# Attention and two feed-forward layers in one kernel: the written-out order of all instructions is replaced by another, and the planner's prices with it

## The chip, the core and the metric

One core of a Trainium2 chip runs one program. The metric is the device time of one execution in microseconds (us). Three executions of the kernel before took 1180.26, 1184.04 and 1186.45 us; the median, 1184.04, is the time before.

## What is computed

Attention over 4 batches of 12 heads, 448 positions, head size 64, with q and k normalised; its output, as 1792 rows of 768, goes through one feed-forward layer (768 to 2048 to 768) and a gated one (768 to 1536 to 768). All inputs and the output are float32.

```python
q_n, k_n = rmsnorm(q, g_q), rmsnorm(k, g_k)
attn = softmax(scale * q_n @ k_n.T)
x = (attn @ v).transpose(0, 2, 1, 3).reshape(B * S, H * D)
h = x @ w_in                       # 1792x768 @ 768x2048
x = (h * sigmoid(h)) @ w_out       # 2048x768
g = x @ w_gate                     # 768x1536
return (g * sigmoid(g) * (x @ w_val)) @ w_out2
```

## The kernel before, in words

Nearly every float32 operand is split into two float16 halves, a high part and a remainder, and a product is three float16 matmuls. Five engines share the work: PE multiplies; ACT, DVE and POOL take exponentials, maxima, splits and scalings; SP issues nearly all DMAs. Weights are loaded, scaled to a power of two and split (`bring`, `split`, `convert`) while attention runs. Attention of the four batches overlaps with the first feed-forward layer of the batch before it (`softmax_pair`, `pv_pair`, `ffn1_h`, `ffn1_o`). The second layer goes over four blocks of rows, of 512, 512, 384 and 384. The first block uses plain products (`ffn2_gv`); the others use a scheme with seven products for eight (`ffn2_seven`), for which sums of weights are made on the chip: `weight_sums` loads pieces of the gate and value weights again from `y2d` (L1281), combines them on DVE (L1288 to L1291), splits them (L967, L979) and stores them to `s2d` (L1293), from which `ffn2_seven` loads them (L1515). `make_parts` does the like for the last weights: loads from `w2d` (L1480), DVE (L1482 to L1489), ACT (L1486, L1491), stores to `t2d` (L1494). Its ACT results go into one buffer, `th`, so that ACT's next L1486 waits until the three stores before it have landed. `ffn2_seven` takes its products from the accumulators with ACT (L1549) and DVE (L1546), applies the gate (L1562 to L1587) and writes halves (L1586, L1589). `ffn2_out` multiplies (L1643), scales and adds (L1652 to L1656) and stores rows (L1668).

Each step is handed to a planner, `Plan.add`, with the engines that may do it, a price in ns on each, what it reads and writes, and a due time. `Plan.emit` then plays the program through at build time: at each moment the engine that is free first takes, of what is ready, the step that is due first, and its instructions are written out in that order. So the order on every engine, and where there is a choice the engine too, is fixed by prices and due times. The chip runs each engine's list in that order and waits on semaphores; it doesn't reorder. A DMA is a `move(hold, service, lead, ...)`: SP is held for `hold`, and the transfer lands after the transfers ahead of it and its own `lead` and `service`. Where the plan leaves PE idle for more than `GAP` ns, it fills the gap with matmuls whose result nobody reads (L1811).

Due times come from formulas plus offsets of a search that was run beforehand and left in `TUNE`: `OFF` by kind of step, `FINE` by one step, `NUDGE` by number of the step. Letters in `TUNE` (`A`, `D`, `P` for ACT, DVE, POOL) say which engines may do a step; where there are several, `emit` picks.

The planner before also knows that PE's instruction stream is fetched in pieces: with `FETCH = (128, 73, 1500.0)` it counts the matmuls that it writes out and, at the 73rd and every 128 after that, makes whatever transfer comes next land 1500 ns later:

```python
if fetches and t0 >= fetches[0]:
    fetches.pop(0)
    served += bump
```

Of the kernel before, what the change touches and what calls it, by code (L numbers as in the profile page):

```python
# [26 lines left out]
    WIY=('DP', 'D', 'AP', 'AP', 'DP', 'ADP', 'AD', 'AP'),  # L27
    WOY=('AD', 'A', 'AD', 'ADP', 'AD', 'D', 'ADP', 'AP'),
# [27 lines left out]
    TK='AD',
    NB=('ADP', 'AD', 'ADP'),
    WIH=('AP', 'A', 'AD', 'DP', 'A', 'AD', 'ADP', 'AP'),
    WIL=('D', 'P', 'E', 'D', 'DP', 'D', 'DP', 'DP'),
    WOH=('D', 'ADP', 'A', 'AP', 'AP', 'ADP', 'ADP', 'AD'),  # L60
    WOL=('E', 'E', 'E', 'E', 'E', 'E', 'E', 'E'),
    WIS=('P', 'P', 'AP', 'P', 'D', 'P', 'A', 'AP'),
    WOS=('D', 'D', 'D', 'D', 'D', 'D', 'D', 'D'),
# [320 lines left out]
def t_ptt(n):  # L384
    return 2.1 * n + 50
# [1461 lines left out]
```

## Time and profile before

| | |
|---|---|
| median of three executions | 1184.04 us (1180.26 to 1186.45) |
| the profiled execution | 1184.59 us, of which the span from first to last instruction 1182.8 |
| busy in the span | PE 1140.7, DVE 917.6, ACT 749.7, POOL 260.6 us |
| mean granted TensorE clock | 0.996 of full speed |
| PE time in matmuls that only fill gaps (L1811) | 24.7 us, 86 of them |
| DMA | 222.59 MB, mean 188 GB/s |

Times are in us from the first instruction unless ns is said. An engine's idle time matters only where it reaches PE, which is busy for 96% of the span; a row's last part in brackets is the idle time of the engine just before it and what ended that.

### The profile page before, as it was taken

The numbers are of one execution on the slowest core, as the hardware profiler recorded it, in microseconds if no ns is written. First come the engines' busy times: TensorE is split into PE (matmuls) and PEld (weight loads), VectorE is DVE, ScalarE is ACT, GpSimd is POOL, SyncE is SP. The second block draws the span as 40 slices with busy tenths as digits, with TensorE's granted clock in tenths as the row PEclk, the third lists the DMA queues.
The fourth block names the chain that finished last, engine by engine and source line by source line (L and its number), as shares of the span: only waits on it lengthen the run. The fifth ranks groups of instructions, "written<-read, shape, count | busy, mean of one in ns | idle before, by whom it ended". The sixth has DMA issues, their size and how long they took to land.

```text
span 1182.8 us, 20080 instructions
## 1 busy us (share of the span) xinstructions
PE 1140.7 (96%) x7400; PEld 675.8 (57%) x7400; DVE 917.6 (78%) x1762; ACT 749.7 (63%) x1288; POOL 260.6 (22%) x231
## 2 busy tenths in 40 slices
PE   8999998999999999999999999999999899999998
PEld 4444544454444445454555554445688668987995
DVE  5989988988588876885379978877999866774773
ACT  4888978887599856995468667574356531441440
POOL 4585222245344524531031021000000000000000
PEclk9999999999999999999999999999999899999999
DMA  9555755689979997776756878646787675463432
GB/s 212 160 132 146 242 202 154 111 193 189 201 158 180 184 203 163 149 139 136 260 176 200 295 250 298 217 157 199 237 255 249 231 247 168 161 190 117 168 130 67
DMA packets 271315, 222.59 MB, mean 188 GB/s; under 512 B 187120, under 2 KB 246000, under 8 KB 271216
## 3 DMA queue, kind: packets, MB, share of 16 engines
q1 hardware_dynamic: 271056, 221.10, 68.0%
q8 instruction: 58, 0.95, 0.3%
q14 instruction: 41, 0.34, 0.1%
q10 hardware_dynamic: 160, 0.20, 0.0%
HBM read 140.44 MB, written 38.14 MB: 151 GB/s over the span
## 4 chain that ended last, share of the span: by engine, by line
PE 34%; DMA 9%; DVE 7%; ACT 5%; issue 2%; SPq 1%; POOL 1%; ACTq 0%; DVEq 0%; POOLq 0%
PE ps L1529 12%; PE ps L1643 9%; PE ps L1155 5%; PE ps L1195 4%; DMA ATT<-y2d 3%; PE ps L1407 2%; DMA ATT<-in_moe_w_out_dram 2%; DMA t2d<-ATT 1%; DMA ATT<-s2d 1%; DMA ATT<-in_moe_w_val_dram 1%; DVE ATT L979 1%; PE ps L951 1%; ACT ATT L1034 1%; DMA ATT<-x2d 1%; PE ps L841 1%
## 5 line engine op out<-in xcount | busy, mean ns | idle before, releaser
L1155 PE MATMUL ps<-XT,W 128*128 128x448 f16 x1152 | 232.5, 352 | 2.5 <-ACT FD L1161 2.3
L1195 PE MATMUL ps<-G,W 128*128 128x448 f16 x1152 | 233.4, 352 | 1.5 <-ACT FD L1199 1.1
L1155 PEld LDWEIGHTS <-W 128*128 128x128 f16 x1152 | 112.0, 98 | 108.1 <-issue 7.9
L1195 PEld LDWEIGHTS <-W 128*128 128x128 f16 x1152 | 111.9, 98 | 108.1 <-issue 6.0
L1529 PEld LDWEIGHTS <-ATT 128*128 128x128 f16 x1458 | 130.8, 99 | 16.4 <-issue 6.5
L1529 PE MATMUL ps<-XT,ATT 128*128 128x192 f16 (+1 forms) x972 | 122.0, 257 | 6.8 <-ACT G L1549 5.7
L860 ACT ACTIVATE ER<-ps,ST 128x448 f32<-128x448 f32 x144 | 102.0, 712 | 12.2 <-DVE ATT L884 5.0
L1643 PEld LDWEIGHTS <-G 128*128 128x128 f16 x720 | 70.3, 98 | 46.9 <-issue 0.3
L1643 PE MATMUL ps<-W,G 128*128 128x384 f16 x528 | 95.8, 326 | 0.1
L851 DVE TENSOR_REDUCE ST<-ps 128x2 f32<-128x896 f32 (+1 forms) x96 | 91.7, 965 | 5.3 <-PE ps L820 2.5
L884 DVE SCALAR_TENSOR_TENSOR ATT<-ER,ST,ATT 128x448 f16<-128x448 f32 x114 | 81.1, 729 | 3.5 <-ACT ATT L876 2.8
L1407 PE MATMUL ps<-XT,W 128*128 128x512 f16 x360 | 81.6, 379 | 1.3 <-ACT FD L1199 0.6
L1529 PEld LDWEIGHTS <-W 128*128 128x128 f16 x810 | 73.0, 98 | 8.3 <-issue 3.1
L1529 PE MATMUL ps<-XT,W 128*128 128x192 f16 (+1 forms) x540 | 73.2, 256 | 2.7 <-DVE ATT L1656 1.8
L1529 PE MATMUL ps<-ER,ATT 128*128 128x192 f16 (+1 forms) x486 | 66.5, 257 | 0.0
L1407 PEld LDWEIGHTS <-W 128*128 128x128 f16 x360 | 35.2, 98 | 43.1 <-issue 3.0
L841 PE MATMUL ps<-ATT 128*128 128x448 f16 x216 | 55.3, 353 | 3.7 <-ACT ER L860 2.9
L694 POOL TENSOR_TENSOR ST<-ST 128x14 f32<-128x14 f32 x20 | 55.9, 2797 | 1.4
L1174 DVE SCALAR_TENSOR_TENSOR G<-FD,ST,G 128x448 f16<-128x448 f32 x64 | 46.7, 743 | 7.0 <-POOL G L1168 4.6
L1546 DVE TENSOR_TENSOR FD<-ps,FD 128x192 f32<-128x192 f32 (+3 forms) x90 | 41.3, 464 | 11.2 <-PE ps L1529 9.2
L1656 DVE SCALAR_TENSOR_TENSOR ATT<-ps,ST,ATT 128x384 f32<-128x384 f32 x46 | 27.6, 614 | 23.9 <-ACT ATT L1652 23.3
L951 PE MATMUL ps<-ATT 128*64 128x448 f16 x396 | 42.2, 355 | 4.0 <-DMA ATT<-ATT 4.0
(283 smaller groups left out, 2123.8 us busy)
## 6 DMA issues: line engine op xcount, KB each, us to landing
ATT<-s2d SPq DMA_DIRECT2D x36, 768.0 KB, 4.3
ATT<-in_moe_w_out_dram SPq DMA_DIRECT2D x24, 768.0 KB, 6.6
ATT<-t2d SPq DMA_DIRECT2D x36, 384.0 KB, 3.6
W<-in_moe_w_in_dram SPq DMA_DIRECT2D x16, 768.0 KB, 6.5
ATT<-in_moe_w_gate_dram SPq DMA_DIRECT2D x12, 768.0 KB, 5.7
ATT<-in_moe_w_val_dram SPq DMA_DIRECT2D x12, 768.0 KB, 5.5
y2d<-ATT SPq DMA_DIRECT2D x24, 384.0 KB, 2.9
ATT<-y2d SPq DMA_DIRECT2D x12, 768.0 KB, 5.8
```

What stands on the lines that cost most here:

```text
L694: op(POOL, 2600, lambda: nc.gpsimd.tensor_tensor(st["r"], st["r"], half, ALU.pow), shared=False, r=["half"], w=[("r", i)], due=due)
L841: nc.tensor.matmul(out=sp[:, u, 0:S], lhsT=T[:, 0, t, :], rhs=T[:, a, :, 64 * h:64 * h + 64], start=(a == 1), stop=(a == 2))
L851: op(DVE, 1.04 * S * nt + 65, lambda sp=sp, top=top, nt=nt: nc.vector.tensor_reduce(top, sp[:, 0:nt, 0:S], AX.X, ALU.max, negate=True), r= ...
L860: op(ACT, 705, lambda e=e, u=u, t=t, sp=sp, own=own: nc.scalar.activation(e, sp[:, u, 0:S], AF.Exp, bias=st["nb"][:, t:t + 1], scale=1.0 i ...
L884: DVE: (t_stt(S), lambda e=e, hi=hi, lo=lo, r1=r1: nc.vector.scalar_tensor_tensor(lo, e, r1, hi, ALU.mult, ALU.subtract), True),
L951: nc.tensor.matmul(out=PS_X[64 * h:64 * h + 64, 0:S], lhsT=vv[:, h, b, :], rhs=PT[:, b].rearrange("p t c -> p (t c)")[:, S * h:S * h + S], ...
L1155: nc.tensor.matmul(out=ps[:, 0:S], lhsT=w[:, a, kk], rhs=xt1((b * HP + kk) % NX, x), start=(kk == 0 and s == 0), stop=(kk == KD - 1 and s ...
L1174: DVE: (t_stt(S), lambda gt=gt, hi=hi, lo=lo, s1=s1: nc.vector.scalar_tensor_tensor(lo, gt, s1, hi, ALU.mult, ALU.subtract), True),
L1195: nc.tensor.matmul(out=ps[:, 0:S], lhsT=w[:, a, P * m:P * m + P], rhs=GV1[:, f, x], start=(f == 0 and s == 0), stop=(f == NF1 - 1 and s == 2))
L1407: nc.tensor.matmul(out=ps[:, 0:n], lhsT=w[:, aa, kk], rhs=xt2(kk, x)[:, 0:n], start=(kk == 0 and s == 0), stop=(kk == KD - 1 and s == 2))
L1529: nc.tensor.matmul(out=ps[:, h * o:h * o + h], lhsT=w[:, aa, kk], rhs=XW[kk][:, c:c + h], start=(kk == 0 and s == 0), stop=(kk == KH - 1 a ...
L1643: nc.tensor.matmul(out=ps[:, bank, 0:384], lhsT=lh[a], rhs=rh[b], start=(x == 0 and (bank, a, b) != (1, 1, 0)), stop=(x == m - 1 and (bank ...
```

## The change

The order is another one. `FINE` and `NUDGE` hold other numbers throughout (the same steps, other due times), and many letters differ. The fetch model is taken out: `FETCH`, the counting of matmuls and the bump are gone, so that the build no longer knows when a fetch comes. The search that found the new numbers was run beforehand, with each candidate judged by ten plays in each of which a tenth of the transfers land late, every transfer in exactly one; none of that search is in the kernel. Nine prices differ. No step of the computation is added or removed, and no wait is added by hand.

```diff
-    FETCH = (128, 73, 1500.0)
...
-                if fetches and t0 >= fetches[0]:
-                    fetches.pop(0)
-                    served += bump
...
-            if e == PE:
-                streamed += self.products[i]
-                while streamed >= fetch:
-                    fetches.append(t0)
-                    fetch += step
...
-        op(POOL, 295, lambda: nc.gpsimd.tensor_scalar(st["r"], ...      # L693, L753
+        op(POOL, 190, lambda: nc.gpsimd.tensor_scalar(st["r"], ...
-            POOL: (t_ptt(448) + 250, ... raw[:, 1], rk3 ...              # L700
+            POOL: (t_ptt(448) - 75, ...
-        op(PE, 440, mm, r=["psz", "id"] + ek, ...                        # L904
+        op(PE, 475, mm, ...
-                op(PE, *((835, scores_0) if n < N0 ...                   # L820
+                op(PE, *((925, scores_0) if n < N0 ...
-            POOL: (t_pts(n) + t_ptt(n) + 96, lo_pool)}), ...             # L974 and L975, in split
+            POOL: (t_pts(n) + t_ptt(n) + 440, lo_pool)}), ...
-        move(420, 2900, 1700, ... in_=y2d ...                            # L1281
+        move(420, 2600, 2650, ...
-        move(490, 1800, 1500, ... out=s2d ...                            # L1293
+        move(490, 1900, 2180, ...
-            move(370, 2300, 2050, ... in_=s2d ...                        # L1515
+            move(370, 2150, 2150, ...
-                move(400, 1300, 1500, ... out=rows, in_=src ...          # L1668
+                move(400, 800, 1540, ...
```

Of the letters, those that the text below speaks of (the others are changed in the same manner):

```diff
-    WOY=('AD', 'A', 'AD', 'ADP', 'AD', 'D', 'ADP', 'AP'),
+    WOY=('AD', 'A', 'A', 'DP', 'ADP', 'ADP', 'D', 'P'),
-    WOH=('D', 'ADP', 'A', 'AP', 'AP', 'ADP', 'ADP', 'AD'),
+    WOH=('AP', 'A', 'A', 'DP', 'ADP', 'A', 'AD', 'AP'),
-    SU='DP',
+    SU='D',
-    TSH='ADP',
-    TSL='A',
-    XU='D',
+    TSH='A',
+    TSL='AP',
+    XU='DP',
```

`TSH` is L1486, `TSL` is L1491, `XU` the additions of L1445, `SU` the remainder of the weight sums (L979 in that place), `WOY` and `WOH` steps of the first output weights.

## Rows read from the trace of the kernel before

**Rows 1.** Busy time by engine in five stretches; then clock, DMA share, GB/s.

```profile
0.00:210.00 210.00, 194.57 (x1005) 95.00 (x1006) 177.27 (x273) 167.31 (x294) 92.80 (x74) 1.00 0.61 176
210.00:500.00 290.00, 280.58 (x1614) 139.63 (x1613) 233.48 (x474) 226.94 (x430) 124.05 (x117) 1.00 0.87 175
500.00:850.00 350.00, 346.90 (x1865) 177.61 (x1864) 266.90 (x495) 227.26 (x335) 43.78 (x40) 1.00 0.70 213
850.00:935.00 85.00, 77.06 (x661) 65.64 (x660) 79.23 (x167) 47.11 (x75) 0.00 (x0) 0.96 0.77 241
935.00:1179.00 244.00, 241.61 (x2263) 197.93 (x2261) 160.45 (x357) 81.09 (x157) 0.00 (x0) 1.00 0.49 162
```

**Rows 2.** PE by line and form: the matmuls that fill gaps.

```profile
L1811 PE MATMUL ps<-NI 128*128 128x512 f16 x86 | 24.7, 412 | 5.1 <-POOL NI L572 5.1
```

**Rows 3.** Timeline of ACT and PE around 920: start, duration, engine, instruction.

```profile
919.79 0.78 ACT L1486 ACTIVATE ATT<-W,ST 128x576 f16<-128x576 f32 x1 [1.43 <-DMA t2d<-ATT]
...
925.10 0.38 ACT L1549 ACTIVATE G<-ps 128x256 f32<-128x256 f32 x1 [0.47 <-DVE W L1580]
...
925.53 0.80 PE L1529 MATMUL ps<-XT,ATT 128*128 128x256 f16 x3 [4.86 <-ACT G L1549]
```

**Rows 4.** DMA view of 914 to 920: queue, and issues with us to landing.

```profile
q8 instruction: 1, 0.02, 1.4%
...
t2d<-ATT SPq DMA_DIRECT2D x3, 96.0 KB, 4.2
```

**Rows 5.** DMA issues of the whole span: count, KB, median us to landing.

```profile
ATT<-y2d SPq DMA_DIRECT2D x12, 768.0 KB, 5.8
s2d<-ATT SPq DMA_DIRECT2D x12, 768.0 KB, 6.7
...
t2d<-ATT SPq DMA_DIRECT2D x36, 96.0 KB, 3.0
...
out_dram<-ATT SPq DMA_DIRECT2D x9, 384.0 KB, 2.8
```

**Rows 6.** DMA queues, whole span: packets, MB, share of 16 engines' span.

```profile
q8 instruction: 58, 0.95, 0.3%
```

**Rows 7.** DMA view of 1080 to 1086: GB/s in 40 slices, queue, issue.

```profile
GB/s 0 0 0 0 0 0 0 0 0 335 348 430 369 369 348 348 21 0 0 0 0 0 20 0 20 0 20 41 20 20 20 0 0 0 0 0 0 0 0 0
...
q8 instruction: 1, 0.02, 1.9%
...
out_dram<-ATT SPq DMA_DIRECT2D x1, 384.0 KB, 4.6
```

**Rows 8.** Timeline of PE, an early and a late stall.

```profile
297.33 0.95 PE L951 MATMUL ps<-ATT 128*64 128x448 f16 x8 [1.22 <-DMA ATT<-ATT]
...
1086.59 0.41 PE L1529 MATMUL ps<-XT,W 128*128 128x192 f16 x3 [1.21 <-DVE ATT L1656]
```

**Rows 9.** DMA view of 293 to 298, its queue row.

```profile
q8 instruction: 1, 0.02, 1.1%
```

**Rows 10.** Busy times and clock of two stretches after that stall.

```profile
925.00:930.00 5.00, 4.46 (x22) 3.08 (x22) 5.00 (x11) 3.15 (x5) 0.00 (x0) 0.50 0.44 160
930.00:935.00 5.00, 5.00 (x41) 4.18 (x40) 3.71 (x8) 1.40 (x2) 0.00 (x0) 0.86 0.48 170
```

**Rows 11.** POOL by line and form: count, busy us, mean ns, idle before.

```profile
L974 POOL TENSOR_SCALAR ATT<-ATT,ST 128x768 f32<-128x768 f32 x6 | 7.6, 1261 | 64.8 <-DVE ATT L968 31.0 <-ACT W L967 12.2 <-DVE W L968 8.1
L975 POOL TENSOR_TENSOR W<-ATT,W 128x768 f16<-128x768 f32 x4 | 7.9, 1986 | 0.3
```

**Rows 12.** POOL's L693 and L700 alone: duration ns min/median/max.

```profile
L693 POOL TENSOR_SCALAR ST<-ST x20: 208/209/1649, 57.7 to 489.5; 128x14 f32<-128x14 f32 x20
...
L700 POOL TENSOR_TENSOR ATT<-ATT,ST x12: 936/1000/1907, 273.3 to 494.1; 128x448 f32<-128x448 f32 x12
```

**Rows 13.** Waits by engine: us in total, times, longest.

```profile
PE ps L795 <- ACT W L798: 4.1, 9, 1.1
PE ps L951 <- DMA ATT<-ATT: 4.0, 4, 1.3
...
ACT ATT L1486 <- DMA t2d<-ATT: 8.7, 4, 6.1
```

More of the change, by code (lines that the diff above doesn't have):

```diff
@@ L145, in __init__ @@
         self.filler = None
-        self.products = {}
     def bank(self, key, ap):
@@ L158, in short, with add @@
         self.drains[j] = i
-    def add(self, alts, r=(), w=(), due=0.0, late=0.0, table=None, cont=False, count=3):
+    def add(self, alts, r=(), w=(), due=0.0, late=0.0, table=None, cont=False):
         i = len(self.ops)
-        self.products[i] = count
         for key in set(r) | set(w):
@@ L241, in emit @@
         served = 0.0
-        step, fetch, bump = self.FETCH
-        streamed, fetches = 0, []
         opened = {}
@@ L332, in emit @@
                     self.fill[i] = 213.0 * times
-                    streamed += times
             if i in self.taken:
@@ L843, in scores @@
                                 rhs=T[:, a, :, 64 * h:64 * h + 64], start=(a == 1), stop=(a == 2))
[L844 to L845 removed]
+                op(PE, *((925, scores_0) if n < N0 else (600, scores_1) if n < HP else (600, scores) if t == J // 2 else (380, scores)),
+                   r=tk, w=[sk[u]], due=due - 1000)
             t0 = tiles[0]
@@ L919, in row_scales @@
         ps, pk = psf()
-        op(PE, 800, lambda: nc.tensor.matmul(out=ps[:, 0:S], lhsT=BO, rhs=DR_0, start=True, stop=True), r=["vl", "vh"], w=[pk], due=due - 500, count=2)
+        op(PE, 800, lambda: nc.tensor.matmul(out=ps[:, 0:S], lhsT=BO, rhs=DR_0, start=True, stop=True), r=["vl", "vh"], w=[pk], due=due - 500)
         rt, rtk = ft()
@@ L936, in pv @@
                             start=(b == 0), stop=(b == 3))
-            op(PE, 3300, pv, r=[(V_0K[n > 0], u) for u in range(3)] + [("pt0", n % 2, t) for t in range(J)], w=["psx"], due=due - 1000, count=16)
+            op(PE, 3300, pv, r=[(V_0K[n > 0], u) for u in range(3)] + [("pt0", n % 2, t) for t in range(J)], w=["psx"], due=due - 1000)
             xf, xk = row_scales(n, due)
@@ L953, in pv @@
                         start=(s == 0), stop=(s == len(steps) - 1))
-        op(PE, 2480, pv, r=["vh", "vl"] + [("PT", t) for t in range(J)], w=["psx"], due=due - 1000, count=22)
+        op(PE, 2480, pv, r=["vh", "vl"] + [("PT", t) for t in range(J)], w=["psx"], due=due - 1000)
         scale = 2.0 ** -14
@@ L1280, in weight_sums @@
         gk, vk, hk, lk = ["Yg"], ["Yv"], ["SHh"], ["SHl"]
-        move(420, 2900, 1700, lambda: nc.sync.dma_start(out=Y.rearrange("p (a c) -> p a c", a=2), in_=y2d[2 * P * f:2 * P * f + 2 * P].rearrange("(a p) c -> p a c", p=P)),
+        move(420, 2600, 2650, lambda: nc.sync.dma_start(out=Y.rearrange("p (a c) -> p a c", a=2), in_=y2d[2 * P * f:2 * P * f + 2 * P].rearrange("(a p) c -> p a c", p=P)),
              r=[("y2d", 2 * f), ("y2d", 2 * f + 1)], w=gk + vk, due=due - 8)
@@ L1292, in weight_sums @@
         split(SH[:, 0:1536], SH[:, 1536:3072], Y, gk + vk, sv, [("sgv", f)], hk, lk, due, 1536, TUNE["SUH"], TUNE["SU"])
-        move(490, 1800, 1500, lambda: nc.sync.dma_start(out=s2d[P * f:P * f + P], in_=SH), r=hk + lk, w=[("s2d", f)], due=due)
+        move(490, 1900, 2180, lambda: nc.sync.dma_start(out=s2d[P * f:P * f + P], in_=SH), r=hk + lk, w=[("s2d", f)], due=due)
         plan.part = None
@@ L1514, in ffn2_seven @@
             sb, sbk = SB[u % 2]
-            move(370, 2300, 2050, lambda sb=sb, f=f: nc.sync.dma_start(out=sb, in_=s2d[P * f:P * f + P]), r=[("s2d", f)], w=sbk, due=t0 + step * (at_f - 2))
+            move(370, 2150, 2150, lambda sb=sb, f=f: nc.sync.dma_start(out=sb, in_=s2d[P * f:P * f + P]), r=[("s2d", f)], w=sbk, due=t0 + step * (at_f - 2))
             z4 = Z[u % 2]
@@ L1667, in store @@
             for rows, src in parts:
-                move(400, 1300, 1500, lambda rows=rows, src=src: nc.sync.dma_start(out=rows, in_=src),
+                move(400, 800, 1540, lambda rows=rows, src=src: nc.sync.dma_start(out=rows, in_=src),
                      r=[("ot", o, 0), ("ot", o, 1)], due=-1e4)
```

80 lines of the change are left out of this document (39 added, 41 removed), and 82 rows, old and new, of the table NUDGE.

## The prediction

> **What bounds the kernel now.** I read the busy times by stretch first. PE is busy 194.57 of 210, 280.58 of 290, 346.90 of 350, 77.06 of 85 and 241.61 of 244 us [rows 1]: it leaves 15.4, 9.4, 3.1, 7.9 and 2.4 idle, 38.3 in all, and nothing but a last store lies behind 1179. The matmuls are the same after the change, so the time can move only by this idle time, by what the clock loses, by the 24.7 us of matmuls that fill planned gaps [rows 2], and by the tail. The largest loss for its length is 850 to 935, where DVE is busy 79.23 of 85 and POOL not at all [rows 1].
>
> Next I read PE's stalls in order of time, and for each of the long ones the chain behind it and the DMA view of the same moment. The longest is 4.86 us, ended at 925.5 by ACT's L1549 [rows 3]. Five microseconds before, ACT had stood 1.43 us at L1486 until stores to `t2d` landed; what follows L1486 in ACT's list, L1549 among it, came late with it, and DVE and ACT then waited for each other in turn. The three stores of that moment took 4.2 us where such stores take 3.0 by the median, and one packet of the instruction queue fell among them [rows 4, 5]. That queue carried 58 packets of 16 KB [rows 6]; 0.3% of 16 engines over 1182.8 us is 56.8 us, about 1 us of one DMA engine for each. What such a packet does is plain at 1080: a store's data run at some 350 GB/s until 1082.5, then at 20 until 1084.7 (slices of 0.15 us), with one packet of the instruction queue in between, and the store takes 4.6 us where its kind takes 2.8 [rows 5, 7]. One engine of 16 was held, and the landing counts only when all are through. PE's 1.21 us stall at 1086.6, released by DVE's L1656, stands behind that store, and its 1.22 us stall at 297.3 behind a DMA, again with an instruction packet just before it [rows 8, 9]. So three stalls of PE, 4.86 + 1.21 + 1.22 = 7.3 us, follow a fetch that met a transfer, although the plan before knew of the fetches.
>
> The long one costs more than its length: after it the granted clock was 0.50 until 930 and 0.86 until 935 [rows 10]. That is 4.46 us of work at 1.2 GHz, and 0.14 / 0.5 of 5, 1.4 us, more; half of 5.9 is 2.9 us lost. The long stall is thus worth 4.86 + 2.9 = 7.8, and the three together 10.2 us.
>
> **The change part by part.** The sum is made against the profiled execution, 1184.6 us (span 1182.8 and 1.8 around it), 0.6 above the median shown.
>
> *The fetch model goes out.* It issues nothing on the chip; what goes is the knowledge of when 58 transfers will be late. What comes in its place is an order chosen to lose little whichever tenth of the transfers is late. I take it that as many fetches as before, three, still reach PE, since the build is now blind to them, but that each costs what the two short ones did, 1.2 us, because an order in which one late transfer idles PE for 4.9 us would have lost in one of the ten plays. That is 3.6 instead of 10.2: minus 6.6. The ends: none reaches PE, minus 10.2; or two long ones and a short one, 16.8, plus 6.6.
>
> The Trainium skill, in "Runtime: NRT & Kernel Launch", section "Instruction fetch mechanics", says that the stream is refilled in 16 KiB blocks and that the crossing is mostly hidden. The size and number agree with the trace; that it is hidden holds for PE's own queue, not for the transfers beside it. By that rule the fetch model would be worth nothing and this term would be its first end, minus 10.2.
>
> *Transfers of the weight sums.* Hold, lead and service of the load from `y2d` sum to 5.67 us instead of 5.02, measured 5.8; of the store to `s2d` to 4.57 instead of 3.79, measured 6.7 [rows 5]. A load that is planned longer is issued earlier or its DVE work is planned later; either way fewer of DVE's steps stand in line before their data. Its worth is in the stretch 850 to 935, where DVE is the busiest: PE's idle time there without the long stall is 7.9 - 4.9 = 3.1 us [rows 1, 3]. I take a third, minus 1.0; the ends are nothing and minus 3.1. The row stores' price falls from 3.20 to 2.74, measured 2.8 [rows 5], and that of the `s2d` loads from 4.72 to 4.67. I take nothing for these two: no instruction comes of them, and PE's idle time after 935, 2.4 us [rows 1], is where a store planned too short would show; at worst it is one more stall like that at 1086, 1.2.
>
> *POOL's prices.* The remainder on POOL, 1261 + 1986 ns for 768 columns [rows 11], was priced 2643 and now 2987; L693 takes 209 and was priced 295, now 190; L700 takes 1000 and was 1241, now 916 [rows 12]. All three are nearer to the rows than before. What they move hides behind PE: up to 850 POOL is busy 43.78 of 350 where PE is busy 346.90 [rows 1]. Value nothing; if that cover were gone, PE's 3.1 us idle there is the most to win.
>
> *Letters.* `XU` and `TSL` let POOL into the stretch where it was not busy at all. Worth nothing to worse: the same L700 took from 936 to 1907 ns [rows 12], so one POOL step between ACT and DVE may be late by 0.9; were all twelve L1491 moved there, 10.9 us of lateness against 85 - 79.2 = 5.8 of DVE's idle leaves plus 5.1. In the other direction L1445's DVE work would go to POOL, which I count inside the third above. I take nothing, since `emit` picks the engine that is done first and ACT is busy only 47.11 of 85.
>
> *The first 210 us.* PE idles 15.4 us there besides the fillers, and the price of scores and transposes and the letters of the first output weights differ. How the search fell out here can't be read from rows. PE's waits for ACT's L798 are the nearest row, 4.1 us [rows 13]: value nothing, ends minus and plus 4.1. The 210 to 500 stretch has the like in PE's waits for transposing DMAs, 4.0 in 4 [rows 13]; one of them is counted above.
>
> Sum: 1184.6 - 6.6 - 1.0 = 1177.0 us.
>
> **The rivals.** *The long stall only moves.* `make_parts` still has twelve L1486 on ACT, each behind the landing of three stores, four of which waited 8.7 us in all, and now `TSH` allows ACT alone, so ACT's list has the same trap [rows 3, 13]. If one fetch, now unforeseen, falls there as before, a short stall becomes a long one: 1177.0 + 7.8 - 1.2 = 1183.6. For it speaks that one of only a few such coincidences did it before; against it that the new order was chosen with such lateness in view.
>
> *Slower: two long stalls.* The same trap springs twice, since the plan no longer steers around fetches: 1177.0 + 2 x 6.6 = 1190.2. It decides from the second long stall on. For it: DVE has 5.8 us of idle time in 85, so lateness there isn't made up [rows 1]; stores with a fetch among them are 1.2 us late [rows 4, 5]. Against it: in the rows of before only one of four L1486 waits reached PE for long.
>
> *The fetch costs nothing.* If transfers come late through wrong prices alone, the better prices remove all three stalls: 1184.6 - 10.2 - 1.0 = 1173.4. For it: the count of late transfers that PE felt is three of 58 fetches. Against it: the tail at 20 GB/s around the fetch at 1081 to 1084.7 [rows 7]. By the rule of the Trainium skill above, this is the time.
>
> *The change does nothing that can be measured,* since the chip's lateness is not the planner's: 1184, inside the first rival's case.
>
> **How the numbers follow.** A measurement of this kernel can tell about 0.5% from no change, 5.9 us: below 1178.1 is faster, above 1190.0 slower. Chances: the forecast 0.44, of which 0.28 lies below 1178.1, since 1177.0 is only a little below that bound; the long stall moves (or nothing happens) 0.20, of which 0.03 falls above 1190.0, when the first 210 us and the stores go wrong too; two long stalls 0.19; the fetch costs nothing 0.17. Faster: 0.28 + 0.17 = 0.45. Same: 0.16 + 0.17 = 0.33. Slower: 0.03 + 0.19 = 0.22. The likeliest case's own range is 1171 to 1182: from 1177.0 two short stalls fewer (2.4) and the rest of the 3.1 (2.1), or 4.1 more in the first 210 us with 1.2 for a store. The range for 8 in 10 must take in both neighbours: low 1168, the third rival with 4.1 better in the first 210 us and a little of the 3.1; high 1191, just past the two long stalls.
>
> **What would show it.** Right: no stall of PE over 3 us between 850 and 935 and a granted clock of 1.00 there; still two to four PE stalls of about 1.2 us behind a transfer with a packet of the instruction queue in it; the count of those packets again 58. Wrong in the first term: a PE stall of 4 to 5 us behind L1486 or another DMA-bound step, with clock 0.50 after it. Wrong in the second: PE as idle as before in 850 to 935 with DVE above 93% busy. Wrong in what I took as nothing: PE idle in 0 to 210, or filler time, different by over 4 us.

## The result, and the profile after

The kernel after took 1190.9 us by the median (1185.45 to 1194.97), the kernel before 1181.6 (1179.14 to 1186.45), ten runs of each: ratio 1.0076 [1.0054, 1.0098], slower by 9.0 us. The profiled execution after took 1194.34 us, with a span of 1192.6. Lines after stand four lower than before: L1486 is L1482 now, L1491 L1487, L1529 L1525, L1549 L1545, L979 L975.

Busy times by stretch after (the first four answer to those of [rows 1], columns as there):

```profile
0.00:210.00 210.00, 193.35 (x993) 94.55 (x994) 179.53 (x272) 161.96 (x275) 80.73 (x69) 0.98 0.59 174
210.00:500.00 290.00, 280.97 (x1605) 141.85 (x1604) 230.46 (x455) 226.15 (x438) 127.14 (x131) 1.00 0.88 177
500.00:850.00 350.00, 348.38 (x1873) 178.67 (x1872) 267.19 (x492) 222.04 (x336) 41.03 (x44) 1.00 0.67 206
850.00:935.00 85.00, 73.30 (x615) 60.75 (x614) 74.25 (x148) 43.71 (x66) 8.15 (x11) 0.96 0.74 238
935.00:1193.00 258.00, 250.09 (x2322) 204.59 (x2321) 169.16 (x372) 84.05 (x163) 5.40 (x8) 0.98 0.50 164
```

Up to 850 PE's busy time is much the same: 1.2 us less in the first stretch, 0.4 and 1.5 more in the next two. In 850 to 935 PE is idle 11.7 us instead of 7.9, although DVE has 5.0 us less to do there. PE's stalls after, from its timeline, and the clock behind the three longest (windows, columns as in [rows 10]):

```profile
95.79 0.96 PE L821 MATMUL ps<-ATT 128*64 128x448 f16 x4 [2.19 <-ACT ER L856]
...
886.15 1.81 PE L1525 MATMUL ps<-XT,ATT 128*128 128x256 f16 x15 [0.86 <-DMA ATT<-s2d]
...
895.08 0.50 PE L1525 MATMUL ps<-XT,ATT 128*128 128x256 f16 x3 [1.27 <-DMA ATT<-s2d]
...
916.82 3.36 PE L1525 MATMUL ps<-XT,ATT 128*128 128x256 f16 x15 [5.06 <-ACT FD L1545]
...
938.06 1.44 PE L1525 MATMUL ps<-XT,ATT 128*128 128x256 f16 x6 [5.15 <-ACT G L1545]
```

```profile
96.00:102.00 6.00, 6.00 (x26) 2.94 (x24) 4.10 (x8) 5.14 (x12) 0.38 (x1) 0.50 0.38 128
...
917.00:923.00 6.00, 6.00 (x37) 4.51 (x36) 5.72 (x14) 2.56 (x5) 0.00 (x0) 0.64 0.61 207
...
938.00:940.00 2.00, 1.94 (x10) 1.34 (x10) 2.00 (x7) 1.59 (x2) 0.51 (x1) 0.50 0.92 332
940.00:945.00 5.00, 5.00 (x40) 4.09 (x39) 4.41 (x7) 0.72 (x1) 0.00 (x0) 0.82 0.43 175
```

Where before had one stall of 4.86 us [rows 3], after has two, 10.2 us together: 5.3 more. The half clock behind them costs 6 x 0.36 + 2 x 0.50 + 5 x 0.18 = 4.1 us, against 2.9 behind the one of before [rows 10]: 1.2 more. These 6.5 us are most of the 9.8 between the two profiled spans; they are what was to be explained. The rest can be placed by counting the columns of the products that PE still has to do (2.4 columns a ns, fillers left out). By that count the new order is 1.6 us behind at 850, 5.1 at 905, 11.2 at 945 and 9.8 at the end. So 3.5 us are lost between 850 and 905, ahead of the long stalls, and there PE waits 0.86 and 1.27 us for loads from `s2d`; in the whole kernel such waits are 2.3 us after and 1.0 before. The experiments were aimed at the two long stalls and left these loads alone.

Packets of the instruction queue are 58 again [rows 6]. The chain of waits through both stalls (start, us, what):

```profile
899.83 4.69 DMA t2d<-ATT
...
904.62 0.78 ACT ATT L1482
...
910.62 4.93 DMA W<-w2d
...
916.38 0.39 ACT FD L1545
...
927.94 1.82 DVE ATT L975
929.78 4.44 DMA ATT<-y2d
...
937.74 0.28 ACT G L1545
```

It has everything in it: stores of `make_parts` that took 4.7 us, a load from `w2d` of 4.9, the weight sums' L975, a load from `y2d` issued 0.1 us after a packet of the instruction queue. The waits and the issues point the same way; ACT's waits at L1482 are three times those of [rows 13], and `t2d` stores take 3.9 us where they took 3.0 [rows 5]:

```profile
ACT ATT L1482 <- DMA t2d<-ATT: 25.1, 6, 7.6
```

```profile
ATT<-y2d SPq DMA_DIRECT2D x12, 768.0 KB, 5.6
s2d<-ATT SPq DMA_DIRECT2D x12, 768.0 KB, 6.1
t2d<-ATT SPq DMA_DIRECT2D x36, 96.0 KB, 3.9
```

### The profile page after: what moved, and what is told of

It is laid out like the page before. It is cut to its first block, busy times and chain, and to the rows that moved or that the text cites. A ratio compares the mean times of both kernels' runs of the same rounds, so it can differ in the third digit from the quotient of the medians.

```text
span 1192.6 us, 20048 instructions
## 1 busy us (share of the span) xinstructions
PE 1146.1 (96%) x7404; PEld 680.4 (57%) x7404; DVE 920.6 (77%) x1735; ACT 737.9 (62%) x1275; POOL 262.4 (22%) x263
## 4 chain that ended last, share of the span: by engine, by line
PE 42%; DMA 6%; DVE 4%; ACT 1%; issue 1%; SPq 0%; POOL 0%; ACTq 0%; DVEq 0%; POOLq 0%
PE ps L1525 13%; PE ps L1639 10%; PE ps L1403 8%; PE ps L1191 7%; PE ps L1151 5%; DMA ATT<-y2d 2%; DMA ATT<-s2d 1%; DMA W<-w2d 1%; DVE ATT L975 1%; DMA s2d<-ATT 1%; DMA ATT<-in_moe_w_gate_dram 1%; DMA ATT<-in_moe_w_val_dram 1%; DMA t2d<-ATT 1%; DMA ATT<-x2d 0%; PE ps L947 0%
## 5 line engine op out<-in xcount | busy, mean ns | idle before, releaser
L1525 PEld LDWEIGHTS <-ATT 128*128 128x128 f16 x1458 | 131.1, 99 | 26.0 <-issue 8.9
L1525 PE MATMUL ps<-XT,ATT 128*128 128x192 f16 (+1 forms) x972 | 123.7, 260 | 13.9 <-ACT FD L1545 5.9
L880 DVE SCALAR_TENSOR_TENSOR ATT<-ER,ST,ATT 128x448 f16<-128x448 f32 x119 | 86.4, 750 | 13.1 <-ACT ATT L872 11.1
L1525 PEld LDWEIGHTS <-W 128*128 128x128 f16 x810 | 72.7, 98 | 6.0 <-issue 1.6
L1525 PE MATMUL ps<-XT,W 128*128 128x192 f16 (+1 forms) x540 | 69.5, 255 | 0.6 <-DVE G L1542 0.6
L1525 PE MATMUL ps<-ER,ATT 128*128 128x192 f16 (+1 forms) x486 | 66.0, 257 | 0.0
L872 ACT ACTIVATE ATT<-ER,ST 128x448 f16<-128x448 f32 x86 | 54.4, 661 | 17.4 <-issue 8.3
L1442 POOL TENSOR_TENSOR ATT<-ATT 128x192 f32<-128x192 f32 (+1 forms) x19 | 16.3, 864 | 170.0 <-DMA ATT<-x2d 120.2
L1157 ACT ACTIVATE FD<-ps,ST 128x448 f32<-128x448 f32 x64 | 39.4, 630 | 18.1 <-PE ps L1151 12.9
```

The lines of the kernel that those rows point to most:

```text
L872: ACT: (t_act(S, False, 1), lambda e=e, hi=hi, r1=r1: nc.scalar.activation(hi, e, AF.Copy, scale=r1)),
L880: DVE: (t_stt(S), lambda e=e, hi=hi, lo=lo, r1=r1: nc.vector.scalar_tensor_tensor(lo, e, r1, hi, ALU.mult, ALU.subtract), True),
L1525: nc.tensor.matmul(out=ps[:, h * o:h * o + h], lhsT=w[:, aa, kk], rhs=XW[kk][:, c:c + h], start=(kk == 0 and s == 0), stop=(kk == KH - 1 a ...
```

## The experiments

Each suspect was taken away on both kernels. In all but the two runs of part 2 the order is frozen: the same step on the same engine at the same place of every list, and only what a step emits is changed. Ratios are to the kernel before, run beside it; 0.0010 is 1.2 us.

### 1. A second buffer for `make_parts`

```diff
+        th_a, th_b = ...      # two pieces of W that nothing uses before the sums of columns 4 and 5
...
+                tt = [(th, slice(0, 3))] if i == 0 else [(th_a, slice(0, 2)), (th_b, slice(2, 3))]
...
-   ... nc.scalar.activation(th[:, :, 0], tf, AF.Copy, scale=sc)
+   ... each(lambda t_, x_: nc.scalar.activation(t_[:, :, 0], tf[:, x_], AF.Copy, scale=sc))
```

> The order, the prices and the letters are those after the change; only every second round of make_parts writes its halves into a second buffer (two pieces of W that nothing uses then), so L1482's successor no longer waits until the three t2d stores of the round before have landed. It costs 18 more short instructions. Theory 1, the single buffer of make_parts makes both long stalls: ACT's waits for DMA at L1482 fall from 25.1 us to under 8, the two stalls of 5.06 and 5.15 us shrink under 2.5 each and their half clock goes, 1190.9 becomes 1178 to 1184. Theory 2, the blindness to fetches makes them: the fetches are where they were, both stalls stay over 4, 1188 to 1193. Theory 3, DVE's load makes them (weight sums of 1.81 us each in its line): stalls over 4, 1189 to 1194, the added instructions cost a little.

> The same edit on the kernel before, with its own order frozen. Theory 1: its one long stall of 4.86 us and the half clock after it go, 1181.6 becomes 1173 to 1177. Theory 2 (the fetch that met the t2d stores at 916.5 would have hit PE with one buffer or two) and theory 3: within 2 us of 1181.6.

Measured: 1.0073 [1.0045, 1.0100] and 0.9985 [0.9965, 1.0005]. The wait is gone, the stalls are not; after, with the buffer (ACT's waits, then PE's timeline):

```profile
ACT ATT L1490 <- DMA t2d<-W: 1.7, 1, 1.7
```

```profile
912.45 2.51 PE L1533 MATMUL ps<-XT,ATT 128*128 128x256 f16 x15 [4.00 <-ACT FD L1553]
...
933.17 1.44 PE L1533 MATMUL ps<-XT,ATT 128*128 128x256 f16 x6 [5.14 <-ACT G L1553]
```

In the kernel before no L1486 waits for a store any more, and the stall is 4.95 us where it was 4.86:

```profile
922.35 2.08 PE L1537 MATMUL ps<-XT,ATT 128*128 128x256 f16 x9 [4.95 <-ACT G L1557]
```

Theory 1, which was mine after reading the two traces, falls: the wait at L1482 ended before another one that is as long.

### 2. The model put back, and taken out

```diff
+    FETCH = (128, 73, 1500.0)      # after, with the counting as before, prices and letters of after
```
```diff
-    FETCH = (128, 73, 1500.0)      # before
+    FETCH = (128, 73, 0.0)
```

> The kernel after the change with the planner's model of fetches put back (every 73 matmul instructions the next transfer is counted 1500 ns late), prices, letters and shifts as after; the order is drawn anew by it. Theory 2: the long stalls go, 1179 to 1184. Theory 1 and theory 3: nothing systematic; another order from shifts that were fitted without the model, 1186 to 1200, and L1482's waits for DMA over 15 us.

> The kernel before with the model's delay set to 0 ns instead of 1500, all else as before; the order is drawn anew. Theory 2: more fetches reach PE, slower by 5 to 10 us, with long stalls behind transfers that hold a packet of the instruction queue. Theory 1: another order from shifts that were fitted to the model, 1182 to 1195, its loss not tied to packets of the instruction queue.

Measured: 1.0521 [1.0492, 1.0551] and 1.0671 [1.0642, 1.0700], far outside what any theory gave. Both orders are drawn anew from shifts that were fitted to other conditions, so these runs don't price the model; they show what a drawing not searched for costs: 4.4 and 6.7% of the kernel that each was drawn from, six to nine times the difference that is asked about. No part of the change (prices, letters, model) can be undone alone and measured, since each one redraws the order. Part of their loss has a familiar place, PE's longest waits of each, the first of the one with the model, the second of the one without:

```profile
PE ps L1539 <- ACT G L1559: 14.9, 3, 7.8
```

```profile
PE ps L1529 <- ACT G L1549: 23.3, 6, 17.0
```

L1539 and L1529 are the products of `ffn2_seven`, L1525 in the kernel after, held by the drain that ACT does.

### 3. The fetches moved

```diff
+            if first and n < 12:      # in the first gap: 48 fillers of 128 columns for 12 of 512
+                for x in range(4):
+                    nc.tensor.matmul(out=ps[:, P * x:P * x + P], lhsT=NI, rhs=NI, start=True, stop=True)
+                continue
```

> The kernel before, its order unchanged; in the first planned gap of PE twelve fillers of 512 columns are given as forty-eight of 128, the same columns in 36 more matmuls, so that every later packet of PE's instruction queue comes about 36 matmuls (half the distance of two) earlier. Theory 2 (a fetch that meets a transfer makes the long stall): no packet falls among the t2d stores at 916 any more, the stall of 4.86 us goes or shows up behind another transfer, 1173 to 1177 or a stall elsewhere. Theory 4 (the stall lies in the order itself: the lists of DVE and ACT before L1549 are longer than PE's work, whatever lands when): a stall of 4.5 to 5.3 us before the same matmul, time within 2 us of the kernel before.

> The same edit on the kernel after the change. Theory 2: the second long stall (its load from y2d was issued 0.1 us after a packet) shrinks by the 1 to 2 us of a fetch or more, the first can do anything; time 1183 to 1195. Theory 4: both long stalls stay at 4.5 to 5.6 us before the same two matmuls, time 1189 to 1193.

Measured: 1.0006 [0.9989, 1.0023] and 1.0082 [1.0055, 1.0110]. In the kernel before, ACT's last two L1486 no longer wait for stores, the stores of 914 land in 1.8 us with no packet of the instruction queue among them, and the stall is there nevertheless, 4.18 us (timelines of ACT and PE, DMA view of 914 to 919):

```profile
918.08 0.78 ACT L1486 ACTIVATE ATT<-W,ST 128x576 f16<-128x576 f32 x1 [1.44 <-DVE W L1484]
...
925.29 0.78 ACT L1486 ACTIVATE ATT<-W,ST 128x576 f16<-128x576 f32 x1
...
931.64 2.08 PE L1529 MATMUL ps<-XT,ATT 128*128 128x256 f16 x9 [4.18 <-ACT G L1549]
```

```profile
q1 hardware_dynamic: 1393, 0.69, 52.3%
...
t2d<-ATT SPq DMA_DIRECT2D x3, 96.0 KB, 1.8
```

Packets meet transfers elsewhere in this run. One falls among the stores of two rounds earlier (in 905 to 908): they take 6.0 us, and ACT waits 0.88 us for them at L1486, where it hadn't waited before. So this run alone doesn't clear the fetches of the long stall; it does so together with the second buffer, with which no L1486 waits for a store and the stall is 4.95 us.

```profile
911.74 0.77 ACT L1486 ACTIVATE ATT<-W,ST 128x576 f16<-128x576 f32 x1 [0.88 <-DMA t2d<-ATT]
```

The two short stalls do answer to the fetches. The store that took 4.6 us at 1080 takes 2.3 at 1085, and no stall of 0.3 us is left in 1070 to 1105; the stall at 297 is 0.70 us instead of 1.22. With the second buffer, where the packets are as before, they are 1.14 and 1.30. (The 36 matmuls are 0.28 of the 128 from one packet to the next, 7400 matmuls for 58 packets, and not half of the distance.)

In the kernel after the packet that preceded the second stall by 3.3 us now precedes it by 9.0, and the stall is 5.15 us as before; the first is 3.96 instead of 5.06, the only trace of theory 2. The chain of that second stall has no transfer in it in this run. The time doesn't follow.

### 4. The stalls filled

```diff
+    MORE = {4559: 42, 4593: 44}      # after; {4593: 40} in before: step of PE's list, matmuls in front of it
...
+        for _ in range(count):
+            nc.tensor.matmul(out=ps[:, 256:512], lhsT=NI, rhs=NI.unsqueeze(1).to_broadcast([P, 2, P]), start=True, stop=True)
```

> The kernel before, its order unchanged; 40 matmuls of 256 columns (107 ns each at 2.4 GHz, 4.3 us) stand in PE's list in front of the matmul that ends the long stall, into the unused half of a bank. What they write is read by nothing. If the half clock after the stall costs what I took for it, 2.9 us: granted clock 1.00 in 925 to 935 and 1178 to 1179.5 against 1181.6. If the clock there is no loss to PE (its work waits for others anyway): within 1 us of 1181.6.

> The kernel after, its order unchanged, with 42 and 44 such matmuls in front of the two matmuls that end its long stalls. By the rows after (0.64 for 6 us, 0.50 for 2 and 0.82 for 5) the clock costs 2.2 + 1.9 = 4.1 us: 1186 to 1188 against 1190.9, and clock 1.00 from 912 to 945. If PE's work waits for others anyway: within 1 us of 1190.9.

Measured: 0.9980 [0.9966, 0.9993], 2.4 us, and 1.0034 [1.0017, 1.0051], 5.0 us under the kernel after. Windows of the kernel before with fillers, which answer to [rows 10]:

```profile
925.00:930.00 5.00, 4.70 (x43) 3.96 (x41) 4.97 (x14) 3.83 (x9) 0.00 (x0) 1.00 0.82 292
930.00:935.00 5.00, 5.00 (x47) 4.41 (x46) 5.00 (x9) 1.67 (x3) 0.00 (x0) 1.00 0.40 166
```

In the kernel after the clock is 1.00 too, in 912 to 945. So the clock is a real part of a stall's price, and by these intervals of about the size that its rows gave. Two more kernels repeat the fills of after, one with the second buffer, one with nine more fillers in front of the early stall:

> The kernel after with the matmuls in front of the two that end its long stalls and the second buffer. If the second buffer is worth as little as in its own run (0 to 2 us): 1185 to 1188, still over the kernel before by 2 to 4 us, which is the length of the second stall. If it helps once the clock is held, as in the kernel before (3 us): 1182 to 1185.

> The kernel after, its order unchanged, with the matmuls in front of the two that end its long stalls, and nine more fillers of 512 columns (1.9 us) in front of the L821 that ends the early stall of 2.19 us at 95.8, after which the clock was 0.50 for 6 us (3 us lost) in the profiled run. If the early half clock belongs to this order in most executions (six of eight traces of it had 0.52 to 0.76 in 95 to 102): 1.5 to 2 us less than with the two fills, ratio 1.0015 to 1.0025. If it only shifts work that waits for transfers later on: 1.0030 to 1.0040, as with two fills.

Measured: 1.0057 [1.0040, 1.0074] and 1.0056 [1.0035, 1.0077]. Against the same kernel without fills, the fills gave 5.0, 1.9 (with the second buffer) and 2.4 us; only the first is clear of the noise, some 3 us for such a difference. The run with the second buffer, 1189.2 us, missed both of its branches: the buffer added nothing to the fills. With the early fill the clock in 95 to 102 was 1.00, but so it was without that fill in two other traces of the new order, and no gain came: 1.0056 against 1.0034. Whether the half clock there costs anything isn't shown. Step 4593 is the same product in both kernels. The planner's own start times, which its list keeps, have a gap of 4.7 us in front of it in the order before, and of 2.9 and 5.8 in front of 4559 and 4593 in the new one; that is a forecast by the planner's prices and no measurement, but it says that the long stalls stood in the plans, with no transfer late. So the stall in front of 4593 is one that both kernels have, and the one in front of 4559, 5.06 us, is what the new order adds.

### 5. DVE's work, stores and loads taken out, one after the other

```diff
-        ... nc.vector.scalar_tensor_tensor(vl, gl, rc, vl, ALU.mult, ALU.subtract)
+        ... nc.vector.scalar_tensor_tensor(vl[:, 0:16], gl[:, 0:16], rc, vl[:, 0:16], ALU.mult, ALU.subtract)
...
-            DVE: (t_stt(n), lambda: nc.vector.scalar_tensor_tensor(dst_lo, src, s, dst_hi, ...), True),
+            DVE: (t_stt(n), (lambda: nc.vector.memset(dst_lo, 0.0)) if plan.tag == "sums" and n == 1536 else ..., True),
```

> The kernel after, its order unchanged. DVE's work on the weights is nearly left out: L1478, L1479, L1480 and L1485 of make_parts and L1284 to L1287 of make_sums do 16 of their columns, and the weight sums' L975 is a memset of the same tile, so the halves and sums of the weights are wrong; every transfer, every step of ACT and every wait stays. Theory 5 (DVE's list is what is too long between 885 and 940: this work stands in it ahead of the steps that free PE's banks): both stalls of 5.06 and 5.15 us shrink under 1.5, 1190.9 becomes 1176 to 1180. Theory 6 (DVE's work is a part only; the rest is the serial chain of FFN2's own steps and of make_parts through ACT and the stores, which stands in the lists as before): the two stalls keep about half, 5 us together, 1184 to 1187. Theory 1 (landings of the stores) and theory 2 (fetches): stalls unchanged, 1189 to 1193.

> The same on the kernel before (same part left out). Theory 5: its stall of 4.86 us goes under 1.5, 1181.6 becomes 1173 to 1176. Theory 6: 2 to 3 us of it stay, 1177 to 1180. Theories 1 and 2: unchanged, 1180 to 1183.

Measured: 1.0041 [1.0026, 1.0056] and 0.9956 [0.9940, 0.9971]. DVE is busy 58.55 of the 85 us after instead of 74.25, and the stalls keep 3.64 + 3.54 us (4.08 in the kernel before):

```profile
913.03 3.36 PE L1526 MATMUL ps<-XT,ATT 128*128 128x256 f16 x15 [3.64 <-ACT FD L1546]
...
933.10 1.44 PE L1526 MATMUL ps<-XT,ATT 128*128 128x256 f16 x6 [3.54 <-ACT G L1546]
```

4.1 and 5.2 us are gained, but the two stalls that theory 5 would have ended are there: it falls, and theory 6 keeps more than the half it gave.

> The kernel after, its order unchanged, with both: DVE's work on the weights nearly left out (as in the run with DVE light, so the weights' halves and sums are wrong) and the second buffer for every second round of make_parts, so that L1482 doesn't wait for the stores. Theory 7 (two chains of nearly equal length run through the stretch, DVE's list and the landings of make_parts' transfers; taking one away leaves the other): the stalls that either edit left, 9.1 us and 7.2 us together, fall under 3 together, 1180 to 1184 on a chip where the kernel before takes 1182 to 1184. Theory 6 (what is left is FFN2's own serial chain): the stalls keep 6 to 7 us together, 1186 to 1189.

> The same two edits on the kernel before. Theory 7: its stall, 4.1 us with DVE light and 4.9 with the second buffer, falls under 1.5, 1173 to 1176. Theory 6: 3.5 to 4 us of it stay, 1176 to 1179.

Measured: 1.0019 [1.0004, 1.0035] and 0.9943 [0.9926, 0.9960]; stalls of 3.25 + 3.69 us and 3.92. Theory 7 falls by the stalls, though in the kernel after the time fell by another 2.6 us, about as much as the noise of such a difference.

```diff
+        m = 768 if loads[0] == 1 else 64
+        nc.sync.dma_start(out=Y...[:, :, 0:m], in_=y2d[2 * P * f:2 * P * f + 2 * P, 0:m]...)
```

> The kernel after, its order unchanged, with DVE's weight work nearly left out, the second buffer, and of the loads from y2d all but the first cut from 768 to 64 of their columns (the sums of the weights are wrong, as before). Theory 8 (what is left are the loads: 768 KB loads of the weight sums crowd the queues, and make_parts' loads of 96 KB take 6 us behind them): the two stalls left with the first two edits, 3.3 and 3.7 us, fall under 1.5 each, 1179 to 1182 where the kernel before takes 1182.5. Theory 6 (what is left is FFN2's own chain, standing in the lists): they stay over 2.5 each, 1184 to 1187.

> The same on the kernel before, whose stall of 3.9 us then stood behind a load from y2d that took 7 us. Theory 8: under 1.5, 1172 to 1175. Theory 6: over 3, 1175 to 1178.

Measured: 1.0005 [0.9994, 1.0017] and 0.9938 [0.9917, 0.9960]. Before, the stall is down to 2.13 us, so a load was a part of it there. After, 3.49 + 3.69 are left. The first then ended with a DMA, a store from the second buffer, so the runs don't say what it would be without one. The second, 3.69 as in the run before, has no transfer in its chain (lines sixteen higher than after: L1498 and L1503 are ACT's two steps of `make_parts`, L1598 and L1561 are L1582 and L1545):

```profile
907.32 12.59 PE ps L1541 x90
919.93 0.70 DVE FD L1558
...
921.29 0.95 ACT W L1498 x2
922.23 0.60 ACT G L1598
922.83 0.67 ACT W L1503 x2
923.49 0.41 ACT W L1598
...
924.33 0.51 ACT ATT L1598
...
924.87 0.56 DVE W L1599
...
927.19 0.28 ACT G L1561
```

From PE's product at 919.9 to the drain at 927.5 stand 7.6 us of short steps of ACT and DVE in a row, `make_parts`' last round (L1498, L1503) among those of `ffn2_seven`; PE had 3.9 us of products in its list for them. That the two sit together has a reason in the code, read from the planner's dependencies and not tried: the marker at the end of `make_parts` frees the room into which L1582 splits its sums for the columns from 2 on, so these can't come before the last round. In the plans of both orders that marker is what the first of them waits for last. The round starts at 919.8 before and at 931.0 after (the twelfth L1486 and L1482).

All this is about the stall that both kernels have. For the one that only the new order has, in front of 4559, the runs say less: there a transfer stands in the chain each time. In the kernel after, with the second buffer, with the fetches moved, and in the first two runs of this part it is a load from `w2d` for `make_parts`, which took 4.6 to 6.4 us. DVE waited 0.81 us for it in the kernel after, so it can have made at most that much of the 5.06; with DVE light the wait is 1.40, with the second buffer too 1.97. No run takes this load away.

```profile
915.65 0.42 DVE L1478 SCALAR_TENSOR_TENSOR W<-W,ST 128x192 f32<-128x192 f32 x1 [0.81 <-DMA W<-w2d]
```

### 6. A version that beats both

> The kernel before with both edits that seemed to help it, its order unchanged: the forty matmuls in front of the matmul that ends its long stall, and the second buffer for every second round of make_parts. If the two add up (2.4 and 1.7 us): 1177 to 1179, ratio 0.9965, under both kernels. If the second buffer's gain was scatter: 1179 to 1181.

Measured: 0.9954 [0.9939, 0.9970], 1177.2 us where the kernel before took 1183.5: the old order, forty fillers and a second buffer. Its stretch, to be held against [rows 1] (fillers count as busy):

```profile
850.00:935.00 85.00, 82.87 (x751) 72.89 (x749) 82.53 (x182) 50.41 (x91) 0.00 (x0) 1.00 0.81 259
```

### What they add up to

The difference between the two orders, after minus before under the same edit: 0.0088 with the second buffer, 0.0076 with the fetches moved, 0.0085 with DVE light, 0.0076 and 0.0067 with the stores' wait and the loads gone too, 0.0054 with the stalls filled, 0.0103 with the stalls filled and the second buffer. Without an edit it is 0.0076. By the intervals of the two ratios each of these is known to 0.002 or 0.003, so none differs clearly from 0.0076. Whatever was taken from both, the distance stayed about where it was. So it is shown that fetches, DVE's weight work, the waits for stores and the loads from `y2d` don't make most of the difference.

The loads from `s2d` and `w2d` were taken from neither kernel. In 875 to 905 PE is busy 26.2 of 30 us after and 29.2 before; with the lists frozen it is at most 27.6 in every other trace of the new order and at least 28.7 in every other of the old. So about 2 us of the distance, by the means, stand in the short stalls ahead of the long ones, which no edit touched.

What is left are the lists themselves: which products PE has in hand while the serial steps run. The plans speak for it: besides the gaps of 2.9 and 5.8 us the new one has one of 2.4 us, 17 us ahead of the first, where the old one has 4.7 and in that neighbourhood nothing over 0.7. That the lists make the difference is thus argued from what was excluded and from the plans, and not shown; no run changed the lists at these places alone. Why the search ended in such a list stays open.

## Why the prediction was wrong

**The step that failed** is "*The fetch model goes out*", and in it the reading that "three stalls of PE, 4.86 + 1.21 + 1.22 = 7.3 us, follow a fetch that met a transfer". For the two short ones the reading holds: they shrank from 1.21 to nothing and from 1.22 to 0.70 us when the packets moved. For the long one it was nearness, not cause: a packet did fall among the stores, and ACT did wait 1.43 us [rows 3, 4], but with the stores ahead of the stall on time it was 4.18 us, and with no wait for stores at all 4.95. The minus 6.6 was drawn from a stall that a late transfer hadn't made, so that nothing spoke for its going. The ten plays with late transfers were no protection: the new plan has its gaps of 2.9 and 5.8 us with no transfer late. Instead of minus 6.6 the runs showed one more long stall, 5.3 us, and 1.2 us of clock.

**The price of a long stall** was about right: I took 4.86 + 2.9 us, the added stall with its clock came to 6.5, and the fills gave 2.4 us of clock back in the kernel before. That two such stalls were forecast at 1190.2 and 1190.9 came is partly luck: the sum started from 1184.6, the kernel before took 1181.6 by the median of ten, and as a difference the forecast was 5.6 us where 9.0 came. And the rival "two long stalls" named the wrong spring: "the plan no longer steers around fetches". Its time came near, its mechanism didn't come true, and 0.19 was too little for a case that needed only another order to be a little worse at one place.

**"The fetch costs nothing"** was right in its premise and wrong in its time. The Trainium skill, "Runtime: NRT & Kernel Launch", section "Instruction fetch mechanics", says that the crossing is mostly hidden. The moved packets agree as far as the whole time goes (1.0006 before, and 1.0082 against 1.0076 after), though one packet cost the store at 1080 about 2 us. I took from it that all three stalls would go, which holds only if fetches or wrong prices had made them.

**Transfers of the weight sums**, minus 1.0, was wrong: without the long stalls PE idles 11.7 - 5.06 - 2.09 (the second's part before 935) = 4.6 us in 850 to 935 where it had idled 3.1. The loads and stores land in 5.6 and 6.1 us, hardly sooner than in [rows 5]. Two of PE's waits there, 0.86 and 1.27 us, are for loads from `s2d`, whose new price I had valued at nothing.

**What I valued at nothing** was otherwise worth little as far as the runs tell: by the count of products left the new order is 1.6 us behind at 850. The first 210 us have a new stall of 2.19 us and a half clock, and filling them gave no gain. POOL took 6.1 us of additions in 850 to 935 (L1445, now L1442), DVE has 5.0 us less there, and PE gained nothing by it; with DVE's weight work gone from both kernels the difference was 0.0085.

**The likeliest case's own range** has a slip: 1177.0 less 2.4 and 2.1 is 1172.5, not 1171. Nothing hangs on it.

**What would show it** was well chosen: PE stalls of 5 us with clock 0.50 after them are what I had named as the sign against the first term. But "behind L1486" would again have led astray; the wait at L1482 was there, 25.1 us in all, and taking it away changed nothing.

## What to carry to other kernels

A late transfer beside a stall is not its cause until the stall goes when the transfer is moved; a few more matmuls early in PE's list move every later fetch, and here the time stayed within 0.2%. One such run isn't enough, since the moved packets meet other transfers. Where a planner draws the order, first ask whether the stall stands in the plan, and try edits that keep the order frozen, since a new drawing alone moves the time by far more than the part that is tried. A stall that can't be removed can at least be filled: forty matmuls into an unused half bank kept the clock and gave 2.4 us.

## What the runs showed that I had not expected

A redrawing with shifts that were fitted to another model costs 4.4 and 6.7%. A single fetch can make a store twice as late, 4.6 us instead of 2.3, and yet moving all 58 of them leaves the time where it was. Filling the long stalls gave 2.4 and 5.0 us; behind the early one, at the same granted clock of 0.50, no gain could be seen. And several chains can be so equally long that each of three suspects, taken away alone, leaves most of the stall: 5.15 us became 5.14 without the wait for stores, 5.15 with the fetch moved and 3.54 with DVE's work gone; it was still 3.69 with DVE's work, the wait for stores and most of the `y2d` loads gone together.
